# Block products from expert 2 of group 2 on: moving a stage border in an attention and mixture-of-experts kernel

## The chip, the cores and the metric

The kernel runs on one NeuronCore of a Trainium2 chip. Five engines work side by side, each through its own queue in order: TensorE (PE) multiplies matrices into PSUM, VectorE (DVE) and ScalarE (ACT) read PSUM and work element by element, GpSimd (POOL) works on SBUF alone, and SyncE (SP) issues DMAs. POOL issues DMAs too, on a queue of its own. The metric is device time in microseconds of one execution. The profile records one further execution of the program.

## What is computed

Attention through 32 memory slots for 8 batches, 8 heads, 576 rows and head size 64; its output, 4608 rows of 512, goes through four experts that are weighted by `domain_probs`:

```python
a = softmax(phi over s)                      # 8, 8, 576, 32
k_m, v_m = a^T k, a^T v                      # 32 x 64 for each head
attn = softmax(q k_m^T / 8 over the 32)      # 8, 8, 576, 32
x = attn v_m                                 # as 4608 x 512
for e in range(4):
    h = maximum(x @ w1[e], 0)                # 4608 x 1024
    out += p[:, e:e+1] * (h @ w2[e])         # 4608 x 512
```

Everything is float32. Each product is made of float32r parts: a number is split into a high part and the rest, and three matmuls (high by high, high by rest, rest by high) make one product.

## The kernel before

**Groups, experts, steps.** The rows are taken in 4 groups of 2 batches (9 tiles of 128 rows), each through 4 experts. The program numbers steps: an expert has `STEPS` = 32 of them, a group `PAIR` = 128. A step is one batch half of a group (256 or 320 rows) and one of the eight 128-wide parts `j` of the hidden size. Counting groups from 0 in the code, group 1 of the code is the second group, "group 2" of the title.

**A step.** `x @ w1` is never formed from x: v_m times w1 is made first (`vw`, 128 x 512 tiles of four heads), then `first` multiplies attention by `vw` (six matmuls, L641 to L643), applies the relu and splits h on ACT and DVE (L653, L655). `second` (L674 to L676) multiplies two row tiles, in every fourth half a third one (`hm`, the middle tile shared by two batches), by w2: three matmuls of 512 columns for each. `first` runs two steps ahead of `second`. `accumulate` adds to `acc` once in eight steps (L694, L696).

**A unit.** From step `BEGIN` on, `unit` takes the place of four steps. Four 128 x 256 blocks of the second product are made by 7 instead of 8 block products. That needs sums and differences of blocks of h (`x_out`, `y_diff`, `y_lo`, `y_last`, from the relu of `rows`, L916 to L918, on ACT, DVE and POOL) and of w2 (`sums`). Each of the 7 (`product`, L1002) is 2 x 3 matmuls of 256 columns; `add_in` (L1020) adds what stands in a product's bank to a quarter of `acc`, seven additions of 128 x 256 in a unit. Two banks (6 and 7) alternate for the products, banks 2 to 5 hold the rows, and two banks (0 and 1, "pm") are left for all else; the steps have four "pm" banks. `middle` (L1040 to L1042) does the shared middle tile as a step does.

**What feeds a unit.** The weights of four units (a block) are 8 tiles of 0.5 MB: four of w2 as split and kept in memory (`kw`), four of sums (`v`). SP loads them (`load_part`, L850) into a ring as the previous block frees its tiles, one in each of the first three units of a block and five in the last. `sums` makes the `v` tiles of one half of an expert: two loads of raw w2 on SP (L201), four operations on DVE a few steps later (L225 to L228), four casts on ACT (L213), four subtractions on POOL (L214) and four stores on POOL's queue (L219). Its raw tile is a buffer that the next job needs as well.

**The plan.** Everything else is hung on steps by `at(step, work)`, and `run_plan` emits it at the start of a step, ahead of that step's products; within an engine that is the order of execution. `ATT` gives each batch the step at which its phi is loaded, the step at which v is written, and the steps of its three score groups and three turns. From the first of these the phi softmax (+3 to +6), its transposes (+8 to +11) and kv products (+10 to +24) follow at fixed distances. A score group is L463 on PE, L473 and L476 on DVE, an exp on ACT and L490 to L493 on DVE; a turn transposes it on PE (L514) and splits it into `AT` (L525, L526). `JOBS` lists the sums: step, home of the raw tile, lag to the DVE part. Where the batches' v lies in memory order for four heads (`vs`), the `vw` of an expert is made for two groups at once (`four`, L579, through three `vst` buffers to `vwd` by POOL's queue, L567) and loaded back (`load_vw`, L618); for experts 1 and 2 of the first two groups it is made in place (`vw_mm`, `vw_out`, L554 and L556). PE, ACT and DVE wait for one another by semaphores; a buffer's next writer waits for its last reader.

The numbers that the change edits:

```python
SEVEN = 2
BEGIN = SEVEN * PAIR
UNITS = (NG - SEVEN) * E * 2 * 4
```

Of the kernel before, what the change touches and what calls it, by code (L numbers as in the profile page):

```python
# [19 lines left out]
P = 128  # L20
# [59 lines left out]
FIRST_LOADS = (PAIR + 112, PAIR + 121, PAIR + 122, PAIR + 123, PAIR + 124, PAIR + 125, PAIR + 126, PAIR + 127)  # L80
# [3 lines left out]
def body(ctx: ExitStack, tc: tile.TileContext, qm, qt, kv, kvt, phi, prob, w1, w1d, w2, out):  # L84
# [104 lines left out]
    def sums(s, home, lag, e, fh):  # L189
# [3 lines left out]
        sub, v = nc.vector.tensor_sub, nc.vector  # L193

# [8 lines left out]
        def high(i, j):  # L203
# [10 lines left out]
            nc.gpsimd.tensor_sub(kept[2][:, i, j], kept[i][:, j], kept[3 + i][:, j].bitcast(F32))  # L214
# [523 lines left out]
    def attention(b, s, written, scores, turns):  # L738
# [43 lines left out]
    for k in range(NG):  # L782
        for e in range(E):
# [38 lines left out]
    for n, job in enumerate(JOBS):  # L822
        sums(*job, n // 2, n % 2)
# [450 lines left out]
```

## Time and profile before

| | |
|---|---|
| time, median of 3 runs | 1392.94 us (1391.73 to 1395.49) |
| the profiled execution | 1392.14 us, of which its span 1390.3 us |
| granted TensorE clock over the span | 0.997 |
| moved by DMA | 301.37 MB, 217 GB/s on average |
| steps 128 to 255 | about 415.5 to 776.6 us of the span |
| first sixteen units | about 776.6 to 936.4 us |

A row of the groups view names line, engine, operation, output and input tiles and their shapes, then busy time and mean duration, then the idle time before and what ended it. A row of the timeline has start, duration, engine, line, operation, and in brackets the wait that went before. The waits view has who waited for what: total us, times, longest.

### The profile page before, as it was taken

To read this page: it belongs to the slowest core of one execution; us is meant where nothing else is said; L and a number is where in the kernel's file an instruction comes from. 1 tells how busy PE (TensorE), PEld (TensorE's weight loads), DVE (VectorE), ACT (ScalarE), POOL (GpSimd) and SP (SyncE) were. 2 spreads that over 40 slices of the span, in tenths; PEclk is the share of its full clock that TensorE was granted. 3 is DMA by queue.
4 is the path that set the end of the run, shared out by engine and by line. 5 is a ranking of instruction groups with operands and counts; after the bars stand their busy time and mean duration, and the time that the engine had idled before them with its cause. 6 is when DMAs were issued, how large, how long until landed. Compare 5 with 4: busy or idle time off the path is not lost.

```text
span 1390.3 us, 25223 instructions
## 1 busy us (share of the span) xinstructions
PE 1362.0 (98%) x8894; PEld 1248.4 (90%) x8894; DVE 841.3 (61%) x1894; ACT 625.4 (45%) x1536; POOL 617.4 (44%) x652
## 2 busy tenths in 40 slices
PE   7999999999999999999999999999999999999998
PEld 6788888788888888889888998999999999999998
DVE  7875535446755365454434467777767666666666
ACT  6765555443345465463344354555543333333332
POOL 4400354745353424433144375677753334443432
PEclk9999999999999999999999999999999999999999
DMA  6742354897675364354598898899984866666661
GB/s 255 240 165 76 117 182 173 311 322 240 210 281 212 107 229 146 125 203 143 178 290 296 277 321 292 286 344 311 326 298 131 259 186 177 180 173 175 175 181 75
DMA packets 102029, 301.37 MB, mean 217 GB/s; under 512 B 24976, under 2 KB 26128, under 8 KB 101904
## 3 DMA queue, kind: packets, MB, share of 16 engines
q1 hardware_dynamic: 81168, 224.26, 51.9%
q0 software_dynamic: 19584, 71.31, 13.0%
q10 hardware_dynamic: 1152, 4.19, 0.7%
q8 instruction: 71, 1.16, 0.3%
q14 instruction: 54, 0.44, 0.1%
HBM read 213.46 MB, written 84.93 MB: 215 GB/s over the span
## 4 chain that ended last, share of the span: by engine, by line
PE 89%; DVE 4%; DMA 2%; issue 2%; ACT 1%; SPq 0%; POOL 0%; DVEq 0%; ACTq 0%; POOLq 0%
PE banks L1002 22%; PE banks L676 9%; PE banks L674 9%; PE banks L675 9%; PE banks L916 5%; PE banks L917 5%; PE banks L918 5%; PE banks L641 5%; PE banks L642 4%; PE banks L643 4%; PE banks L579 3%; PE banks L463 2%; PE banks L357 2%; DMA stage<-in_w 1%; PE banks L1040 1%
## 5 line engine op out<-in xcount | busy, mean ns | idle before, releaser
L1020 DVE SCALAR_TENSOR_TENSOR acc<-banks,pt,acc 128x256 f32<-128x256 f32 x416 | 200.0, 481 | 107.7 <-PE banks L1002 104.2
L160 POOL TENSOR_TENSOR w<-stage,w 128x512 fp32r<-128x512 f32 x134 | 177.0, 1332 | 188.7 <-ACT w L159 179.4
L655 DVE SCALAR_TENSOR_TENSOR h<-banks,h 128x256 fp32r<-128x256 f32 x256 | 107.3, 420 | 168.6 <-ACT h L653 111.4
L676 PE MATMUL banks<-w,h 128*128 128x512 f32 x512 | 201.2, 393 | 3.4 <-DVE h L655 3.4
L674 PE MATMUL banks<-w,h 128*128 128x512 f32 x512 | 201.9, 394 | 0.1
L675 PE MATMUL banks<-w,h 128*128 128x512 f32 x512 | 201.4, 393 | 0.0
L653 ACT ACTIVATE h<-banks 128x256 fp32r<-128x256 f32 x256 | 98.0, 384 | 199.8 <-PE banks L643 169.9
L641 PE MATMUL banks<-AT,vw 128*128 128x256 f32 (+1 forms) x512 | 156.6, 306 | 3.7 <-DVE h L655 1.8
L1002 PE MATMUL banks<-w,a 128*128 128x256 f32 x1080 | 154.4, 282 | 0.3 <-DVE acc L1020 0.2
L643 PE MATMUL banks<-AT,vw 128*128 128x256 f32 (+1 forms) x512 | 150.9, 295 | 1.2 <-DVE vw L556 1.2
L916 PE MATMUL banks<-AT,vw 128*128 128x256 f32 (+1 forms) x512 | 151.6, 296 | 0.0
L642 PE MATMUL banks<-AT,vw 128*128 128x256 f32 (+1 forms) x512 | 151.3, 296 | 0.0
L917 PE MATMUL banks<-AT,vw 128*128 128x256 f32 (+1 forms) x512 | 151.1, 295 | 0.0
L918 PE MATMUL banks<-AT,vw 128*128 128x256 f32 (+1 forms) x512 | 150.9, 295 | 0.0
L1002 PEld LDWEIGHTS banks<-w,a 128*128 128x128 f32 x1080 | 143.6, 188 | 4.8 <-issue 0.9
L983 POOL TENSOR_TENSOR vt<-ph,vt 128x512 fp32r<-128x512 f32 x64 | 84.1, 1314 | 107.3 <-ACT vt L982 78.3
L676 PEld LDWEIGHTS banks<-w,h 128*128 128x128 f32 x512 | 96.3, 188 | 25.8 <-DVE h L655 4.3
L346 POOL TENSOR_TENSOR kvs<-stage,kvs 128x512 fp32r<-128x512 f32 x58 | 75.4, 1317 | 93.2 <-ACT kvs L345 87.3
L641 PEld LDWEIGHTS banks<-AT,vw 128*128 128x128 f32 x512 | 96.8, 189 | 13.8 <-DVE vw L556 3.8
L674 PEld LDWEIGHTS banks<-w,h 128*128 128x128 f32 x512 | 96.4, 188 | 12.0 <-ACT h L653 0.4
L675 PEld LDWEIGHTS banks<-w,h 128*128 128x128 f32 x512 | 96.4, 188 | 10.9
L159 ACT CAST w<-stage 128x512 fp32r<-128x512 f32 x168 | 102.7, 619 | 4.5 <-DMA stage<-in_w 2.1
(149 smaller groups left out, 2985.4 us busy)
## 6 DMA issues: line engine op xcount, KB each, us to landing
w<-kw SPq DMA_DIRECT2D x93, 512.0 KB, 5.5
vwd<-vst POOLq DMA_DIRECT2D x80, 512.0 KB, 6.4
vw<-vwd SPq DMA_DIRECT2D x320, 128.0 KB, 6.0
w<-v SPq DMA_DIRECT2D x55, 512.0 KB, 5.6
stage<-in_w SPq DMA_DIRECT2D x44, 512.0 KB, 4.5
stage<-in_w1d SPq DMA_DIRECT2D x40, 512.0 KB, 5.3
stage<-in_kv SPq DMA_DIRECT2D x32, 512.0 KB, 4.3
kw<-w POOLq DMA_DIRECT2D x24, 512.0 KB, 5.6
```

Of the source, the lines that this page charges most:

```text
L160: eng.tensor_sub(dst[:, 1, :], raw, dst[:, 0, :].bitcast(F32))
L641: nc.tensor.matmul(ps, w[:, 0, f], at_t[:, g, 0, c], start=g == 0, stop=False)
L642: nc.tensor.matmul(ps, w[:, 0, f], at_t[:, g, 1, c], start=False, stop=False)
L643: nc.tensor.matmul(ps, w[:, 1, f], at_t[:, g, 0, c], start=False, stop=g == 1)
L674: nc.tensor.matmul(po[t], x[:, 0, :], w[:, 0, :], start=j == 0, stop=False)
L675: nc.tensor.matmul(po[t], x[:, 0, :], w[:, 1, :], start=False, stop=False)
L676: nc.tensor.matmul(po[t], x[:, 1, :], w[:, 0, :], start=False, stop=j == NJ - 1)
L916: nc.tensor.matmul(ps, w[:, 0, f], at_t[:, g, 0, c], start=g == 0, stop=False)
L917: nc.tensor.matmul(ps, w[:, 0, f], at_t[:, g, 1, c], start=False, stop=False)
L918: nc.tensor.matmul(ps, w[:, 1, f], at_t[:, g, 0, c], start=False, stop=g == 1)
L1002: nc.tensor.matmul(ps, a[:, l, jj], w[:, r, c], start=start and jj + i == 0, stop=jj == 1 and i == 2, skip_group_check=True,)
L1020: VE.scalar_tensor_tensor(a, src, p, a, ALU.mult, ALU.add)
```

## The change

Units begin at step 192 (`PAIR + 2 * STEPS`, expert 2 of the second group) and not at 256: 80 units instead of 64. The attention of batches 4 to 7 has its phi and kv parts packed into steps 122 to 189; the scores of batches 4 and 5 come after it, among the units. The sums of experts 2 and 3 are made first; one job moves to step 74, where its subtractions are on DVE and not on POOL (`BUSY_POOL`), none is left at 119 or 154, and three stand at 190, 202 and 214, with the raw tile in an "AT" buffer. The last folds of batch 7 and the last `vw` tiles of the steps get tables of their own, and a tile that folds still need is taken for the units later (`open_last`).

```diff
 ATT = {
...
-    4: (PAIR + 2, PAIR + 37, (PAIR + 34, PAIR + 37, PAIR + 41), (PAIR + 38, PAIR + 42, PAIR + 45)),
+    4: (PAIR - 6, PAIR + 21, (PAIR + 69, PAIR + 81, PAIR + 85), (PAIR + 99, PAIR + 103, PAIR + 107)),
+    5: (PAIR + 8, PAIR + 35, (PAIR + 109, PAIR + 115, PAIR + 119), (PAIR + 117, PAIR + 123, PAIR + 127)),
...
-SEVEN = 2
-BEGIN = SEVEN * PAIR
-UNITS = (NG - SEVEN) * E * 2 * 4
+SEVEN = 1, 2
+BEGIN = SEVEN[0] * PAIR + SEVEN[1] * STEPS
+UNITS = (LAST - BEGIN) // 4
...
 JOBS = (
-    (62, "", 5), (86, "", 5), (97, "", 5), (108, "", 5), (119, "", 5),
-    (PAIR + 26, "AT", 4), (PAIR + 61, "a", 4), (PAIR + 87, "", 5),
+    (2, 0, 62, "", 5), (2, 1, 74, "", 5), (3, 0, 86, "", 5), (3, 1, 97, "", 5), (0, 0, 108, "", 5),
+    (0, 1, PAIR + 62, "AT", 4), (1, 0, PAIR + 74, "AT", 4), (1, 1, PAIR + 86, "AT", 4),
 )
+BUSY_POOL = (74,)
...
-FIRST_LOADS = (PAIR + 112, PAIR + 121, PAIR + 122, PAIR + 123, PAIR + 124, PAIR + 125, PAIR + 126, PAIR + 127)
+FIRST_LOADS = (-16, -7, -6, -5, -4, -3, -2, -1)
+LAST_PAIR_AT = (28, 29, 31, 32)
+LAST_FOLD = (PAIR + 56, PAIR + 61)
...
+        rest_on = nc.vector if s in BUSY_POOL else nc.gpsimd
...
-            nc.gpsimd.tensor_sub(kept[2][:, i, j], kept[i][:, j], kept[3 + i][:, j].bitcast(F32))
+            rest_on.tensor_sub(kept[2][:, i, j], kept[i][:, j], kept[3 + i][:, j].bitcast(F32))
...
-            for j in range(NJ if 0 < nk < SEVEN else 0):
+            for j in range(NJ if nk and s + STEPS < BEGIN else 0):
                 at(s + W2_AGAIN + j, lambda a=(nk, ne, j): load_w2(*a))
...
-                    when = VW_LOAD_AT if nk < SEVEN else VW_LOAD_7
+                    when = VW_LOAD_AT if s < BEGIN else VW_LOAD_7
...
+    def open_last():
         n = att.tile([P, 2 * P], F32, name="xs", tag="xs", bufs=2)
         ph2["n"] = n.rearrange("p (j c) -> p j c", j=2)
...
-        idle["pm"] = deque(range(2))
+        held_now = [n for tag, n, _ in lent.values() if tag == "pm"]
+        assert not set(held_now) & {2, 3}
+        idle["pm"] = deque(n for n in idle["pm"] if n < 2)
+        open_last()
```

Three places of the instruction queues show it. On PE, in expert 3 of the second group, before (a step; `w` is a tile of w2, `h` the relu's split):

```order
L643 MATMUL banks<-AT,vw 128x256
L674 MATMUL banks<-w_6901,h 128x512
L675 MATMUL banks<-w_6901,h 128x512
L676 MATMUL banks<-w_6901,h 128x512
L641 MATMUL banks<-AT,vw 128x256
```

and among the units of the same group now (`a` is the input of two of the seven products, L923 to L925 are the rows):

```order
L1009 MATMUL banks<-w_6200,a 128x256 x3
L1009 MATMUL banks<-w_6233,a 128x256 x3
L1009 MATMUL banks<-w_5732,a_6400 128x256 x3
L1009 MATMUL banks<-w_6026,a_6400 128x256 x3
L923 MATMUL banks<-AT,vw 128x256
L924 MATMUL banks<-AT,vw 128x256
```

Three matmuls of 512 columns for a row tile have given way to sixes of 256 columns.

On DVE, the first score group of batch 4, before, between steps (`mx` and `z` are its maximum and sum, `at` its softmax, `h` what the next `second` needs):

```order
L473 TENSOR_REDUCE mx<-banks 128x16
L476 TENSOR_TENSOR at<-banks,mx 128x512
L309 TENSOR_TENSOR a<-banks,a 128x2x4x64
L655 SCALAR_TENSOR_TENSOR h<-banks,h 128x256
L309 TENSOR_TENSOR a<-banks,a 128x2x4x64
```

and now the same group in a unit:

```order
L477 TENSOR_REDUCE mx<-banks 128x16
L480 TENSOR_TENSOR at<-banks,mx 128x512
L1027 SCALAR_TENSOR_TENSOR acc<-banks,pt,acc 128x256
L987 SCALAR_TENSOR_TENSOR a<-banks,a 128x512
L1027 SCALAR_TENSOR_TENSOR acc<-banks,pt,acc 128x256 x2
L997 SCALAR_TENSOR_TENSOR xs<-banks,ph 128x256
```

Behind the softmax there now stand the additions that empty the products' banks, and the splits for the next unit, where the split of `h` and of the phi transposes stood.

On POOL, around step 81, before (`vwd` stores a `vst` tile, `w` is a split of w1):

```order
L567 DMA vwd_2966<-vst 128x1024
L160 TENSOR_TENSOR w_2973<-stage,w_2973 128x512
L567 DMA vwd_2996<-vst 128x1024
L160 TENSOR_TENSOR w_3005<-stage,w_3005 128x512
L567 DMA vwd_3028<-vst 128x1024
L160 TENSOR_TENSOR w_3035<-stage,w_3035 128x512
```

and now:

```order
L571 DMA vwd_3008<-vst 128x1024
L163 TENSOR_TENSOR w_3017<-stage,w_3017 128x512
L223 DMA v_3020<-sv 256x1x512
L223 DMA v_3020<-raw 256x1x512
L571 DMA vwd_3046<-vst 128x1024
L163 TENSOR_TENSOR w_3053<-stage,w_3053 128x512
L571 DMA vwd_3088<-vst 128x1024
L163 TENSOR_TENSOR w_3097<-stage,w_3097 128x512
L223 DMA v_3100<-sv 256x1x512
L223 DMA v_3100<-raw 256x1x512
```

Two pairs of stores of the sums (`sv` and `raw` hold the parts) stand between the stores of the four-head products.

More of the change, by code (lines that the diff above doesn't have):

```diff
@@ L187, in load_w2, with sums @@
         w2t[k, e, j] = t
-    def sums(s, home, lag, e, fh):
+    def sums(e, fh, s, home, lag):
         kept = []
@@ L760, in attention @@
             at(s + 13 + 3 * hp, lambda hp=hp: kv_out(b, hp))
-        for g in range(2):
-            at(s + 18 + 6 * g, lambda g=g: [kv_fold(b, 2 * g + i) for i in range(2)])
-            at(s + 19 + 6 * g, lambda g=g: kv_pick(b, g))
+        for g, n in enumerate(LAST_FOLD if b == B - 1 else (s + 18, s + 24)):
+            at(n, lambda g=g: [kv_fold(b, 2 * g + i) for i in range(2)])
+            at(n + 1, lambda g=g: kv_pick(b, g))
         at(written, lambda: v_split(b))
@@ L810, in body @@
                 for odd in range(2 if by_four else 0):
-                    when = VW_LOAD_AT if nk < SEVEN else VW_LOAD_7
+                    when = VW_LOAD_AT if s < BEGIN else VW_LOAD_7
                     at(s + when[odd][fh], lambda a=(nk, ne, odd, fh): load_vw(*a))
                 for g in range(0 if by_four else 2):
+                    when = LAST_PAIR_AT if fh and s + STEPS == BEGIN else PAIR_AT[fh]
                     for i, u in enumerate(units_w1(ne, fh, g)):
                         at(s + PAIR_W1[fh][2 * g + i], u)
-                        vw_steps(s + PAIR_AT[fh][2 * g + i], nk, ne, fh, 2 * g + i, (0, 1))
+                        vw_steps(s + when[2 * g + i], nk, ne, fh, 2 * g + i, (0, 1))
     for b in range(2, B):
@@ L821, in body @@
             at(e * STEPS + KEEP_AT[e] + j, lambda a=(e, j): keep_w2(*a))
-    for n, job in enumerate(JOBS):
-        sums(*job, n // 2, n % 2)
+    for job in JOBS:
+        sums(*job)
     for s in FIRST_LOADS:
-        at(s, lambda: load_part(wp.tile([P, 2, DM], F32R, name="w2", tag="w2", bufs=NJ + 1)))
+        at(BEGIN + s, lambda: load_part(wp.tile([P, 2, DM], F32R, name="w2", tag="w2", bufs=NJ + 1)))
     early = [("kv", 0, 0), ("kvt", 0)] + [("kv", 0, hp) for hp in range(1, NP)]
@@ L842, in parts, with place_of @@
             yield ("v", e, fh, i), (2 + i // 2, i % 2)
+    def place_of(u):
+        k, r = divmod(u + BEGIN // 4, 2 * E * 4)
+        e, r = divmod(r, 8)
+        fh, pair = divmod(r, 4)
+        return k, e, fh, pair // 2, pair % 2
     for block in range(UNITS // 4):
-        e, fh = divmod(block % (2 * E), 2)
+        _, e, fh, _, _ = place_of(4 * block)
         waiting += [(block, *x) for x in parts(e, fh)]
@@ L861, in free @@
                 ring.extend(W[u // 4][i, jj] for jj in range(2))
-    def place_of(u):
-        k, r = divmod(u, 2 * E * 4)
-        e, r = divmod(r, 8)
-        fh, pair = divmod(r, 4)
-        return SEVEN + k, e, fh, pair // 2, pair % 2
     ph2 = {}
```

5 lines of the change are left out of this document (2 added, 3 removed).

## The prediction

> **What bounds the kernel now.** I read the page first: busy time by engine, then the shares of the chain that ended last.
>
> ```profile
> PE 1362.0 (98%) x8894; PEld 1248.4 (90%) x8894; DVE 841.3 (61%) x1894; ACT 625.4 (45%) x1536; POOL 617.4 (44%) x652
> PE 89%; DVE 4%; DMA 2%; issue 2%; ACT 1%; SPq 0%; POOL 0%; DVEq 0%; ACTq 0%; POOLq 0%
> ```
>
> TensorE (PE) is busy 98% of the span of 1390.3 us and carries 89% of the chain. Its busy time isn't yet its peak, so the second view is the windows of the stages that the change touches. The rows are steps 128 to 191 and 192 to 255 of the plan, the first sixteen of the block-product units, and four units without attention.
>
> ```profile
> core 0: us, PE busy (x) PEld busy (x) DVE busy (x) ACT busy (x) POOL busy (x), PEclk, DMA share, GB/s
> 415.50:605.60 190.10, 186.56 (x1074) 163.60 (x1073) 93.79 (x227) 98.97 (x258) 75.09 (x64) 1.00 0.49 171
> 605.60:776.60 171.00, 171.00 (x960) 149.99 (x959) 80.12 (x188) 66.76 (x186) 58.19 (x60) 1.00 0.72 226
> 776.60:936.40 159.80, 158.00 (x1165) 151.01 (x1164) 112.30 (x250) 79.87 (x176) 106.51 (x120) 1.00 0.90 306
> 1102.20:1137.70 35.50, 35.50 (x279) 34.99 (x278) 23.11 (x53) 11.95 (x29) 14.06 (x16) 1.00 0.68 202
> ```
>
> In steps 192 to 255 PE never rests: 171.00 of 171.00 us. This is the stage that is rewritten. It can get shorter only by fewer or narrower matmuls. VectorE (DVE) has room there (80 of 171 us); a quiet unit uses 23.11 of 35.50 us, 65%. So the price of a matmul is the first term, and DVE the first suspect for what comes back.
>
> **What a matmul costs.** The timeline of PE gives starts; neighbouring starts give the price, since a matmul's own length overlaps the next.
>
> ```profile
> 705.85 0.40 PE L674 MATMUL banks<-w,h 128*128 128x512 f32 x1
> ...
> 707.22 0.28 PE L641 MATMUL banks<-AT,vw 128*128 128x256 f32 x1
> 1130.56 0.88 PE L1002 MATMUL banks<-w,t 128*128 128x256 f32 x6
> 1131.27 0.88 PE L1002 MATMUL banks<-w,tl 128*128 128x256 f32 x6
> ...
> 1132.69 1.60 PE L1002 MATMUL banks<-w,a 128*128 128x256 f32 x12
> 1134.13 0.28 PE L916 MATMUL banks<-AT,vw 128*128 128x256 f32 x1
> ```
>
> Six matmuls of 512 columns stand between 705.85 and 707.22 (L674 to L676, twice): 1.37 / 6 = 0.228 us. Six of 256 columns take 0.71 us, 0.118; twelve take 1.44 us, 0.120. I use 0.119. A narrow one costs 52% of a wide one, not 50%.
>
> **Part 1: the products.** Sixteen groups of four steps become sixteen units. Four steps hold 4 x 2 x 3 = 24 wide matmuls; a unit holds 7 x 6 = 42 narrow ones. The first product and the shared middle tile keep their matmuls. So 16 x 24 = 384 wide ones go (384 x 0.228 = 87.6 us) and 16 x 42 = 672 narrow ones come (672 x 0.119 = 80.0 us): **-7.6 us**. With 0.118 and 0.120 at the ends: -8.3 to -7.0. All of it lies on the path, as PE has no rest there.
>
> The TensorE page of the Trainium skill (TensorE: Matmul & The Clock Gate, section "Wait — 56ns, not 53.3ns?") makes a warm matmul N / 2.4 GHz plus 2.5 ns; by that estimate 384 x 215.8 ns go and 672 x 109.2 ns come, -9.5 us. The rows here are 6 to 9% dearer than that at both widths, and the sum goes by the rows.
>
> **Part 2: a wait that goes.** Of the idle 3.5 us in steps 128 to 191, the waits and the timeline name this:
>
> ```profile
> PE banks L641 <- DVE h L655: 1.8, 1, 1.8
> PE banks L641 <- DVE vw L556: 1.7, 3, 0.9
> 516.45 0.39 PE L641 MATMUL banks<-AT,vw 128*128 128x256 f32 x1 [1.83 <-DVE h L655]
> ```
>
> At 516 us, step 162, batch 4's first scores, batch 5's exp and normalisation, the w2 sums loaded at step 154 and the vw tiles of the next expert all stand on DVE and ScalarE within three steps. Afterwards the scores stand at 197 and later, and these sums at 190 or later. The stretch from 121 to 189 has the same phi and kv work per step as before, no scores and no sums. I take **-1.8 us**; ends 0 (something else is late there) and -3.5 (the three vw waits go too, which I don't expect: vw tiles are written at the same steps but two).
>
> **Part 3: scores inside units.** Batches 4 and 5 now do their six score groups and six turns among units 1 to 15. What a group costs there is shown by batches 6 and 7, whose scores already stand in units (840 to 1070 us). First PE's waits, then those of its weight loads:
>
> ```profile
> PE banks L1002 <- DVE acc L1020: 1.9, 4, 1.2
> PE banks L463 <- DVE AT L526: 0.3, 1, 0.3
> PEld banks L1002 <- DVE acc L1020: 2.6, 3, 1.5
> PEld banks L1002 <- issue: 0.7, 2, 0.4
> PEld banks L463 <- DVE AT L526: 0.5, 1, 0.5
> PEld banks L463 <- DVE accm L1052: 0.3, 1, 0.3
> PEld banks L1040 <- DVE at L476: 0.2, 1, 0.2
> ```
>
> Behind a waiting matmul stands the whole PE queue: a product's bank must be emptied by an accumulation on DVE, and that stands behind softmax. Two batches cost 2.2 us of PE idle, or 4.3 us counted at the weight loads. The new two get the same six groups: **+3.0 us**, ends 2.2 and 4.3. Their turns stand 4 or more steps after the softmax (group 3 of batch 6 has one step), which speaks for the middle and not the upper end.
>
> **Part 4: sums inside units.** Three of the eight jobs now run in units 0 to 7, none before. Durations, of DVE, by line:
>
> ```profile
> L493 DVE TENSOR_TENSOR at<-at,z 128x512 f32<-128x512 f32 x16 | 14.8, 922 | 0.4
> L476 DVE TENSOR_TENSOR at<-banks,mx 128x512 f32<-128x512 f32 x16 | 11.0, 690 | 0.5
> L473 DVE TENSOR_REDUCE mx<-banks 128x16 f32<-128x512 f32 x16 | 10.9, 682 | 1.4 <-PE banks L463 1.4
> L490 DVE TENSOR_REDUCE z<-at 128x16 f32<-128x512 f32 x16 | 10.8, 676 | 0.5 <-ACT at L483 0.5
> L226 DVE TENSOR_TENSOR raw<-raw 128x512 f32<-128x512 f32 x8 | 7.5, 936 | 0.3
> ```
>
> A score group is about 0.68 + 0.69 + 0.68 + 0.92 = 3.0 us of DVE and costs 3.0 / 6 = 0.5 us of PE; a job is four operations of 0.7 to 0.9 us, about 3.2 us, in two pairs. So 0.35 to 0.5 each: **+1.0 us** for three, ends 0 and 1.6. DVE itself isn't full: in 16 units 16 x 23.11 / 4 = 92 us, plus 6 x 3.0, plus 3 x 3.2, plus six AT subtractions of about 0.7 (as L476) and the 16 vst subtractions that move along, also 0.7: some 135 us in about 160. That is more than the 112 us of 159.8 in the windows row above, and the rival below.
>
> **Part 5: the job at step 74.** It is new in the stretch in which the four-head products go to memory (steps 72 to 87). It adds four casts on ScalarE, eight operations on DVE (its four low parts are on VectorE there) and four stores on POOL's queue, each ahead of a vwd store. That queue once cost PE this, shown by the waits of ScalarE and by windows:
>
> ```profile
> ACT vst L584 <- DMA vwd<-vst: 15.4, 5, 7.5
> 268.70:271.60 2.90, 0.42 (x2) 0.00 (x1) 0.69 (x1) 1.41 (x5) 0.21 (x1) 1.00 0.93 380
> 271.60:275.80 4.20, 3.55 (x11) 2.98 (x12) 2.54 (x7) 3.09 (x9) 4.16 (x5) 0.59 0.56 113
> 297.70 1.29 POOL L160 TENSOR_TENSOR w<-stage,w 128x512 fp32r<-128x512 f32 x1 [1.60 <-ACT w L159]
> ```
>
> A vst buffer (there are three) was free only after 7.5 us; PE idled about 2.5 of 2.9 us, then ran at a granted clock of 0.59 for 4.2 us (4.2 x 0.41 = 1.7). So 4.2 us is the upper end. At steps 80 to 84 POOL rests 1.60 us of each 3.4 us step, and two more issues fit in that; a 7.5 us wait gave 2.5 us of idle, so 5 us are absorbed. I take **0**, ends 0 and 4.2. The new raw load on SP stands among w1d loads which wait for POOL longer than it does; it hides there.
>
> The SBUF page of the Trainium skill (SBUF — State Buffer, section "Who interferes with whom") says that a VectorE operation with two SBUF inputs blocks against a GpSimd operation reading SBUF, for the whole instruction. L493 and L226, which have such inputs, average 922 and 936 ns against 690 ns of L476, whose input is PSUM, so the trace agrees; by it the four subtractions moved to VectorE at step 80 would take up to 4 x 1.3 us (one POOL operation each) longer, which the 5 us still cover.
>
> Other edits (the second kv fold of batch 7 one step earlier, the last two vw tiles one step later, the "n" tile opened later, first loads by offset, 32 more weight loads of 0.5 MB on SP against 16 w2 reloads gone): 0, hidden as long as PE has rows and products queued; the DMA share of 0.90 in 776 to 936 us, with PE busy 158.00 of 159.80, is the row for that load.
>
> **Sum**, against the profiled execution's own 1392.14 us (span 1390.3, 1.84 around it; the median of the runs, 1392.94, is 0.06% off): -7.6 - 1.8 + 3.0 + 1.0 + 0 = -5.4, so **1386.7 us**.
>
> **Rivals.**
>
> *The step-74 job repeats the vst stall* (Part 5's upper end): -5.4 + 4.2 gives 1391. For: three buffers, and two stores ahead of a vwd store. Against: the rest on POOL.
>
> *DVE fills in units 0 to 15*: 135 us in 160 leaves 15%, and where softmax, sums and a vst subtraction meet, the accumulation is late at each. If each of six groups and three jobs costs 1 us, Parts 3 and 4 are +9 instead of +4: 1391.7.
>
> *SP stands still behind a sums load; slower.* A raw tile can be loaded only when the previous job's stores have landed:
>
> ```profile
> SPq L201 <- DMA v<-raw: 39.5, 4, 17.8
> ```
>
> Four times SP waited, 9.9 us on average and 17.8 at most. In units the same SP queue loads the product weights behind that, at the end of every fourth unit, about one unit (9 us) ahead of use. The loads at steps 202 and 214 come three steps (7 us) after the previous store is issued. Should SP wait more than 9 us there, PE idles for the rest: two waits of 17.8 give 2 x 8.8 = 17.6, so -5.4 + 17.6 = 1404. Here the gap is three steps and not one, so I hold it unlikely.
>
> *Weight loads set the spacing; slower.* If a narrow matmul cost over 87.6 / 672 = 0.130 us, Part 1 would turn sign; at the 0.188 us that a weight load lasts (L1002 PEld below) it is +39, so 1429.
>
> ```profile
> L1002 PEld LDWEIGHTS banks<-w,a 128*128 128x128 f32 x1080 | 143.6, 188 | 4.8 <-issue 0.9
> ```
>
> The starts above exclude it: 0.118 to 0.120. The same TensorE page, section "Back-to-back issue gap", gives 81 ns at 128 and 131 ns at 512 columns for load and matmul pairs; on a line between these 256 columns are an estimated 98 ns, and the change would add 15 us. The trace disagrees with both figures.
>
> *More waits go*: the vw waits too (-1.7) and Parts 3 and 4 at their lower ends (+2.2): 1383.
>
> **Chances.** Forecast 0.55, step-74 stall 0.14, full DVE 0.15, SP 0.07, weight loads 0.01, more waits go 0.08. Within 0.3% of 1392.9 means 1388.8 to 1397.1, about what a measurement of this kernel can tell from no change. Faster: 0.55 and 0.08, less a little at the forecast's edge, 0.61. Same: 0.14 + 0.15 and that edge, 0.31. Slower: 0.08. The range takes in the unknown costs' ends and the two rivals near 1391, and leaves out the SP case: 1381 to 1393.
>
> **What would show it.** Part 1: units 0 to 15 at 42 products each, the quiet ones in about 8.9 us; part 2: no wait of L641 on h near step 162; parts 3 and 4: L1002's successor waiting for the accumulation, 3 to 5 us in the first sixteen units; part 5: no wait of PE in steps 80 to 88. A slow clock, a product waiting for a weight DMA, or PE idle over 5 us in units 0 to 15 would make the prediction wrong.

## The result: slower by 21.5 us, and the profile after

| | before | after |
|---|---|---|
| median (4 runs each, side by side) | 1392.69 us (1391.73 to 1395.49) | 1414.22 us (1413.12 to 1415.76) |
| ratio, with its 95% interval | 1 | 1.0152 (1.0134 to 1.017) |
| profiled execution | 1392.14 us | 1414.01 us |
| granted TensorE clock over the span | 0.997 | 0.992 |

The forecast was 1386.7 us, with a range up to 1393. The busy times and the chain of the changed kernel come first, as they did before:

```profile
PE 1366.3 (97%) x9182; PEld 1260.9 (89%) x9182; DVE 894.7 (63%) x1996; ACT 647.2 (46%) x1552; POOL 669.9 (47%) x712
PE 82%; DVE 7%; DMA 5%; ACT 2%; issue 2%; POOL 1%; SPq 1%; DVEq 0%; ACTq 0%; POOLq 0%
```

PE carries 82% of the chain and no longer 89%; DVE, DMA and ACT took the rest. The windows of the same stages (steps 128 to 191, units 0 to 15, the next sixteen units; columns as before: start and end, length, then PE, its loads, DVE, ACT, POOL, granted clock, DMA share, GB/s) tell where:

```profile
422.00:616.00 194.00, 188.61 (x1079) 164.23 (x1078) 87.12 (x219) 102.92 (x273) 72.66 (x59) 1.00 0.43 144
616.00:790.90 174.90, 162.23 (x1183) 153.82 (x1182) 126.27 (x275) 77.21 (x171) 101.87 (x113) 0.98 0.74 249
790.90:951.00 160.10, 157.73 (x1180) 151.25 (x1180) 116.68 (x260) 79.27 (x178) 109.03 (x123) 1.00 0.95 322
```

Steps 192 to 255 took 171.00 us without a rest. The sixteen units in their place take 174.90 us, of which PE rests 12.7, at a mean clock of 0.98. The units after them are as long as they were (160.10 for 159.80 us).

To split this further, the start of each matmul is set against the next one's, and the median of its line and width is taken off: what is left is lost to waits and to a slow clock. The sums in us, each stage counted from the product that `first` makes for its first step, which runs two steps ahead (so that 128 to 135 in the table is done while the plan is at steps 126 to 133), or from the first rows of its first unit (192 to 203 in the table are units 0 to 2, and so on; below, stretches of steps and units are counted in this way):

| steps | before | after |
|---|---|---|
| start, 0 to 3 | 2.0 | 4.2 |
| 76 to 91 | 5.1 | 7.9 |
| 92 to 107 | 2.3 | 3.8 |
| 128 to 135 | 0.7 | 4.0 |
| 136 to 191 | 3.6 | 3.9 |
| 192 to 203 | 0 | 8.3 |
| 204 to 267 | 0.3 | 13.2 |
| all others | 12.6 | 12.9 |
| **sum** | **26.6** | **58.2** |

So 31.6 us more are lost. PE's own work fell: by the medians 384 wide matmuls of 0.231 went and 672 narrow ones of 0.118 came, -9.4 us. Together that makes 22.2 us, where the two profiled executions are 21.9 us apart. Two rows are taken as chance: in the other kernels that were run the start lost 2.0 to 2.7, and steps 92 to 107 lost about 2.3 or about 3.8, with or without the change.

PE's waits between 600 and 800 us (who waited for whom: us, times, longest; before there was none from 605.6 to 776.6 us):

```profile
PE banks L923 <- DVE v L400: 3.7, 1, 3.7
PE banks L1009 <- DVE acc L1027: 3.6, 7, 1.4
PE banks L583 <- POOL w L163: 2.1, 1, 2.1
PE banks L467 <- DVE AT L530: 1.8, 1, 1.8
PE banks L1009 <- issue: 1.4, 2, 1.2
```

Rows of the first unit wait for batch 7's fold, products for the accumulation, a four-head product for GpSimd, scores for a turn. The experiments take them one by one.

### The profile page after: what moved, and what is told of

Same layout as the page of the kernel before. It is cut to its first block, busy times and chain, and to the rows that moved or that the text cites. A ratio compares the mean times of both kernels' runs of the same rounds, so it can differ in the third digit from the quotient of the medians.

```text
span 1412.2 us, 26074 instructions
## 1 busy us (share of the span) xinstructions
PE 1366.3 (97%) x9182; PEld 1260.9 (89%) x9182; DVE 894.7 (63%) x1996; ACT 647.2 (46%) x1552; POOL 669.9 (47%) x712
## 4 chain that ended last, share of the span: by engine, by line
PE 82%; DVE 7%; DMA 5%; ACT 2%; issue 2%; POOL 1%; SPq 1%; DVEq 0%; ACTq 0%; POOLq 0%
PE banks L1009 26%; PE banks L680 6%; PE banks L678 6%; PE banks L679 6%; PE banks L923 6%; PE banks L924 5%; PE banks L925 5%; PE banks L645 3%; PE banks L646 3%; PE banks L647 3%; PE banks L467 2%; PE banks L583 2%; PE banks L361 2%; PE banks L1047 1%; PE banks L1048 1%
## 5 line engine op out<-in xcount | busy, mean ns | idle before, releaser
L1027 DVE SCALAR_TENSOR_TENSOR acc<-banks,pt,acc 128x256 f32<-128x256 f32 x528 | 253.5, 481 | 131.9 <-PE banks L1009 127.1
L163 POOL TENSOR_TENSOR w<-stage,w 128x512 fp32r<-128x512 f32 x134 | 177.8, 1338 | 154.3 <-ACT w L162 142.0
L1009 PE MATMUL banks<-w,a 128*128 128x256 f32 x1344 | 193.3, 282 | 1.0 <-DVE acc L1027 0.7
L923 PE MATMUL banks<-AT,vw 128*128 128x256 f32 (+1 forms) x640 | 190.2, 297 | 3.7 <-DVE v L400 3.7
L924 PE MATMUL banks<-AT,vw 128*128 128x256 f32 (+1 forms) x640 | 189.6, 296 | 0.0
L925 PE MATMUL banks<-AT,vw 128*128 128x256 f32 (+1 forms) x640 | 189.4, 296 | 0.0
L1009 PEld LDWEIGHTS banks<-w,a 128*128 128x128 f32 x1344 | 179.2, 189 | 6.8 <-issue 1.8
L680 PE MATMUL banks<-w,h 128*128 128x512 f32 x384 | 151.8, 395 | 4.0 <-DVE h L659 4.0
L678 PE MATMUL banks<-w,h 128*128 128x512 f32 x384 | 152.3, 397 | 1.2 <-ACT h L657 0.7
L679 PE MATMUL banks<-w,h 128*128 128x512 f32 x384 | 151.4, 394 | 0.0
L975 ACT ACTIVATE a<-banks 128x512 fp32r<-128x512 f32 x80 | 47.9, 599 | 174.1 <-DVE ph L981 131.3
L923 PEld LDWEIGHTS banks<-AT,vw 128*128 128x128 f32 x640 | 121.1, 189 | 4.6 <-issue 4.1
L1000 POOL TENSOR_TENSOR tl<-xs,tl 128x256 fp32r<-128x256 f32 x80 | 59.7, 747 | 131.8 <-ACT tl L999 66.6
L924 PEld LDWEIGHTS banks<-AT,vw 128*128 128x128 f32 x640 | 121.3, 190 | 0.1
L925 PEld LDWEIGHTS banks<-AT,vw 128*128 128x128 f32 x640 | 121.0, 189 | 0.0
L645 PE MATMUL banks<-AT,vw 128*128 128x320 f32 (+1 forms) x384 | 117.9, 308 | 2.0 <-DVE vw L560 1.9
L1009 PE MATMUL banks<-w,vt 128*128 128x256 f32 x768 | 113.8, 280 | 4.2 <-DVE acc L1027 2.9
L647 PE MATMUL banks<-AT,vw 128*128 128x320 f32 (+1 forms) x384 | 113.2, 296 | 1.3 <-DVE vw L560 1.3
```

Of the source, the lines that this page charges most:

```text
L163: eng.tensor_sub(dst[:, 1, :], raw, dst[:, 0, :].bitcast(F32))
L645: nc.tensor.matmul(ps, w[:, 0, f], at_t[:, g, 0, c], start=g == 0, stop=False)
L647: nc.tensor.matmul(ps, w[:, 1, f], at_t[:, g, 0, c], start=False, stop=g == 1)
L678: nc.tensor.matmul(po[t], x[:, 0, :], w[:, 0, :], start=j == 0, stop=False)
L679: nc.tensor.matmul(po[t], x[:, 0, :], w[:, 1, :], start=False, stop=False)
L680: nc.tensor.matmul(po[t], x[:, 1, :], w[:, 0, :], start=False, stop=j == NJ - 1)
```

## The experiments

Each kernel ran beside the kernel before; compared are the ratios to it (its own median lay between 1392.7 and 1394.3 us from one set of runs to the next) and the lost time by the table's rows. The changed kernel's ratio is 1.0152.

### The packing alone

```diff
-SEVEN = 1, 2
+SEVEN = 2, 0
```

> The changed kernel's attention and sums places, but units only from step 256, as before: the packing alone. Theory A (the packing costs in the steps, at 74 to 104 and 121 to 160): lost time up to step 192 stays as in the changed kernel, about 8 us over before without the start, so 1399 to 1402 us. Rival (the steps swallow it, and the whole loss is made by units from 192 on): 1392 to 1395 us.

Measured: 1401.13 us, ratio 1.0041 (1.0026 to 1.0057). Steps 76 to 91 lost 7.0 and 128 to 135 lost 3.7 us, and from 192 to 267 only 0.2. So the packing costs 0.4%, in two places ahead of 192, and the rest of the loss, 1.1%, is made by the units from 192 on, where the same work stands among units.

### Batch 4's phi

On SP's queue the changed kernel loads phi among the reloads of w2, and DVE stands for it (start, length, engine, line, and in brackets the wait ahead):

```profile
408.81 3.84 SPq L189 DMA_DIRECT2D w<-kw  x3
412.83 1.79 SPq L264 DMA_DIRECT2D ph<-in_phi  x2
...
422.75 0.75 DVE L269 TENSOR_REDUCE nm<-ph 128x1 f32<-128x576 f32 x1 [2.49 <-DMA ph<-in_phi]
...
424.60 0.75 DVE L269 TENSOR_REDUCE nm<-ph 128x1 f32<-128x576 f32 x1 [0.91 <-DMA ph<-in_phi]
...
426.05 0.50 PE L539 MATMUL banks<-w,vt 128*128 128x512 f32 x1 [1.81 <-DVE h L659]
```

The load was issued at 412.83, and its first half was there at 422.75, ten microseconds later, behind three reloads of 0.5 MB. The relu's split stands behind that maximum on DVE, a vw matmul waits for the bank.

```diff
-        at(s, lambda: load_phi(b))
+        at(s - 3 if b == 4 else s, lambda: load_phi(b))
```

> The changed kernel with batch 4's phi loaded at step 119 and not at 122, ahead of the eight w2 reloads on SP's queue instead of among them; nothing else moves. Theory A (the 1.8 us wait at 424 us, and those behind it, come from phi landing 10 us after its issue, so that DVE stands at the maximum ahead of the relu's split): lost time of steps 126 to 133 falls from 4.0 to about 1 us, the median by 3 to 1411 us. Rival (the vw tiles and phi need DVE at once, whenever phi lands): lost time stays above 3 us, 1414 us.

Measured: 1409.6 us, ratio 1.0113 (1.0094 to 1.0132). The same DVE row, now without a wait:

```profile
404.26 1.26 SPq L264 DMA_DIRECT2D ph<-in_phi  x1
...
417.53 0.75 DVE L269 TENSOR_REDUCE nm<-ph 128x1 f32<-128x576 f32 x1
```

Steps 128 to 135 lost 0.8 us for 4.0: the late load was the cause, worth 3.2 us by lost time.

### The job at step 74

```diff
     for job in JOBS:
-        sums(*job)
+        if job[:2] != (2, 1):
+            sums(*job)
```

> The changed kernel without the sums job at step 74: the sums of the second half of expert 2 are not made, and the units load the first half's in their place. Theory A (the job's stores and casts repeat the vst stall): the 5.2 us that PE loses in steps 80 to 83 go, the 5.3 us of before come back in steps 76 to 79 instead of 1.9, so about 2 to 3 us less, 1411.5 us. Rival (the stall belongs to the four-head products alone and moves by itself): 1414, within 1 us of the changed kernel.

Measured: 1408.57 us, ratio 1.011 (1.008 to 1.014). Steps 76 to 91 lost 2.7 us for 7.9. One profile says little here, since this stall varies: in the twelve profiles of kernels with the job these steps lost 6.9 to 8.9 us, 7.8 on average, and in the eight without it 2.6 to 6.9, 4.8 on average. The job costs 3.0 us on average. The ratio fell by more, 0.42% or 5.9 us, but its interval for the kernel without the job, four runs from 1405.9 to 1413.0 us, is wide.

### The border: four orders

The first theory was that batch 7's fold, whose bank the rows of the first unit need, comes too late. First the fold and all of batches 6 and 7 were put two steps earlier:

```diff
-    6: (PAIR + 24, PAIR + 51, ...
+    6: (PAIR + 22, PAIR + 49, ...
-    7: (PAIR + 38, PAIR + 64, ...
+    7: (PAIR + 36, PAIR + 62, ...
-LAST_FOLD = (PAIR + 56, PAIR + 61)
+LAST_FOLD = (PAIR + 54, PAIR + 59)
```

> The changed kernel with the phi and kv parts of batches 6 and 7 two steps earlier, so that batch 7's last fold stands at step 187 and its pick at 188, not 189 and 190. Theory A (the 3.7 us wait of the rows at the border, and the slow clock behind it, come from that pick being late): 3.7 + 1.6 to 3.2 us go, 1408 to 1409 us, and no wait of the rows on v in the trace. Rival (the queues of DVE and ACT are full there whatever stands in them, and the vw tile or the first unit's splits are late next): at least 1412 us.

Measured: 1415.53 us, ratio 1.0148 (1.0124 to 1.0172). The theory fell. The rows wait as before, for the next in line:

```profile
PE banks L923 <- DVE vw L560: 2.8, 1, 2.8
```

Of 8.3 us lost in units 0 to 2, 5.9 stayed, and 3.4 more were lost in steps 136 to 191, into which batches 6 and 7 are now packed more closely. Then the vw tiles were moved as well, in two ways:

```diff
-LAST_PAIR_AT = (28, 29, 31, 32)
+LAST_PAIR_AT = (26, 27, 29, 30)
...
```

> The kernel with batches 6 and 7 two steps earlier, and in addition the last four vw tiles at steps 186, 187, 189 and 190 (not 188, 189, 191 and 192), the last two in banks 0 or 1, which the units keep: neither a fold nor a vw tile then holds a bank that the first unit's rows need. Theory A (the border costs what meets at it): the 3.0 us wait of the rows and most of the 1.5 us one behind goes, with the slow clock, 4 to 6 us less than 1415.5: about 1410.5 us. Rival (ScalarE's first casts for the units, behind which the rest stands, set the border): 1414 us or more.

Measured: 1424.18 us, ratio 1.0215 (1.0189 to 1.0242), with 12.9 us lost in steps 136 to 191 and 10.2 in units 0 to 2. Part of it was a flaw of the edit: at 186 and 187 the previous pair's tiles stand already, so two shared a step.

```diff
-LAST_PAIR_AT = (28, 29, 31, 32)
+LAST_PAIR_AT = ((18, 19, 25, 26), (27, 28, 29, 30))
...
```

> Batches 6 and 7 two steps earlier, and the last six vw tiles one a step: 185, 186, then 187 to 190 (not 186, 187, then 188, 189, 191, 192), the one at 190 in bank 0 or 1. No two tiles share a step, no fold or vw tile holds a bank of the first unit's rows, and only one vw tile is written after the first unit's casts. Theory A: the 3.0 us wait of the rows, the 1.5 us in unit 0 and the slow clock go, 4 to 6 us less than 1415.5: about 1410.5 us. Rival (any vw tile beside the first unit's casts on ACT and DVE costs its 3 us): 1414 us or more.

Measured: 1419.19 us, ratio 1.0186 (1.0168 to 1.0204): without the flaw still worse than with the tiles where they were (1415.53), with 12.9 us lost in units 0 to 2. In both, the last vw matmul waits for the bank that the tile before it holds (4.2 us in the first of the two):

```profile
PE banks L539 <- DVE vw L560: 4.2, 1, 4.2
```

So neither the fold nor a tile was the cause by itself; each is only what stands last. What stands ahead of them shows in the timeline of ScalarE at the border of the changed kernel, and of those who wait for it:

```profile
617.59 0.60 ACT L957 ACTIVATE ph<-banks 128x512 f32<-128x512 f32 x1 [2.37 <-PE banks L925]
618.22 0.41 ACT L966 CAST a<-ph 128x256 fp32r<-128x256 f32 x1
618.68 0.41 ACT L969 CAST t<-ph 128x256 fp32r<-128x256 f32 x1
619.11 1.17 ACT L558 CAST vw<-banks 64x512 fp32r<-64x512 f32 x2
620.18 0.42 ACT L398 COPY kT<-banks 64x64 f32<-64x64 f32 x2
620.62 0.42 ACT L398 COPY v<-banks 64x64 f32<-64x64 f32 x2
...
618.22 0.42 DVE L965 SCALAR_TENSOR_TENSOR ph<-banks,ph 128x256 f32<-128x256 f32 x1 [2.54 <-ACT ph L957]
620.31 1.39 DVE L560 TENSOR_TENSOR vw<-banks,vw 64x512 fp32r<-64x512 f32 x2 [1.67 <-ACT vw L558]
...
622.08 0.45 DVE L400 TENSOR_TENSOR v<-v,banks 64x64 f32<-64x64 f32 x2
...
622.68 0.36 PE L923 MATMUL banks<-AT,vw 128*128 128x256 f32 x1 [3.73 <-DVE v L400]
```

ScalarE stands 2.37 us for the first unit's first rows, since the relu of these rows (L957) was emitted ahead of the work of step 190. The vw casts and the fold's copies stand behind it, though PE had done the matmuls that they read by 614.1 us. VectorE stands as well, 2.54 us for that relu (L965, also emitted ahead of step 190's work) and then 1.67 for the vw cast, and PE waits for banks until 622.68. Its clock pays once more:

```profile
624.00:626.50 2.50, 2.50 (x11) 2.21 (x10) 0.52 (x2) 0.60 (x1) 0.00 (x0) 0.52 0.00 0
```

After 3.73 us of rest the granted clock was 0.52 in this stretch, and its matmuls take the longer for it. The last edit changes only where the first unit's X is made: the relu and two casts on ScalarE, and with them the operation L965 on VectorE and two subtractions on GpSimd:

```diff
-        x_relu(0)
-        x_out(0)
         steps(BEGIN - 2, BEGIN - 1)
+        x_relu(0)
+        x_out(0)
```

> The changed kernel with one thing in another order: the first unit's relu and casts of X (L957 to L970) are emitted behind step 190's work and not ahead of it, so that ScalarE does that step's vw casts and the fold's copies while it would wait for the first rows. Theory C (the rows' 3.7 us wait at 618.6 us comes from ScalarE standing 2.4 us for the first rows with those casts queued behind; border and border2 put more casts into that queue and got worse): the wait falls under 1 us and the slow clock behind it goes, 4 to 5.5 us less, 1409 to 1410 us. Rival (the chain of casts for the first unit is the length that counts, one step later it keeps the first product waiting instead): 1413 us or more.

Measured: 1407.97 us, ratio 1.0113 (1.0091 to 1.0135). The waits of PE from 605 to 660 us and the clock of the first units are now:

```profile
PE banks L1009 <- DVE acc L1027: 2.0, 4, 1.4
...
612.80:628.00 15.20, 13.81 (x92) 12.59 (x91) 10.75 (x24) 8.50 (x21) 5.42 (x7) 1.00 0.43 151
```

No wait of the rows is left, and the clock stays at 1.00. Units 0 to 2 lost 3.0 us for 8.3. This order at the border was worth 5.3 us; ScalarE's and VectorE's share of it are not separated, as both stood for the same rows. Of the 3.0 left, 1.4 are one wait behind a vw tile, and about 1 is the first sums job, as the next kernel suggests, in which the border keeps the order of the changed kernel.

### Sums and scores among units

```diff
     for job in JOBS:
-        sums(*job)
+        if job[2] < PAIR:
+            sums(*job)
```

> The changed kernel without the three sums jobs at 190, 202 and 214: the sums of the second half of expert 0 and of expert 1 are not made, and those of expert 0's first half are loaded in their place. As the prediction had it (0.35 to 0.5 us each): about 1 us less, 1413. Theory A (the third job holds POOL when the four-head products begin at 224, 2.2 us, and DVE's share comes on top): 3 to 4 us less, 1410.5, and no wait of the four-head product on POOL. Rival (the scores fill DVE, the jobs are nothing): 1414.

Measured: 1408.4 us, ratio 1.0101 (1.0074 to 1.0128). The wait for POOL is gone, 1.0 us less is lost in units 0 to 2 and 3.8 less in units 3 to 18: 4.8 us for three jobs, where the prediction had 1.0.

```diff
+        if b in (4, 5):
+            at(scores[0], lambda: st.update({("AT", b): st["AT", b - 2]}))
+            return
         for t0, n in zip((0, 2, 4), scores):
```

> The changed kernel without scores and turns of batches 4 and 5: the units of the third group take the attention of batches 2 and 3. PE's own work falls by 2 x (20 x 0.111 + 10 x 0.11) = 6.6 us. As the prediction had it (3.0 us of waits): 1414.2 - 9.6 = 1404.5 us. Theory A (9.4 us lost in units 3 to 18 beside the jobs' share, nearly all by these scores beside the four-head products): 13 to 15 us less, 1400 us. Rival (the units lose this time by themselves): 1407.

Measured: 1394.51 us, ratio 1.0012 (0.9997 to 1.0027). Units 3 to 18 lost 4.7 us for 13.2. The expectation counted PE's own work too low: a score matmul shows twice, so a batch has 40 of 0.111 and 10 transposes of 0.11 us, 11.1 for two. The rest, 8.5 us, is time lost to waits and to the slow clock behind them (units 12 to 15 lost 0.1 us for 6.6), which the six groups and turns make and for which the prediction had 3.0.

Part of this comes from GpSimd; how much is not separated. Rows of DVE and GpSimd in unit 13 of the changed kernel:

```profile
756.44 2.21 DVE L495 TENSOR_SCALAR z<-z 128x16 f32<-128x16 f32 x1
...
756.62 1.31 POOL L163 TENSOR_TENSOR w<-stage,w 128x512 fp32r<-128x512 f32 x1
757.87 0.74 POOL L967 TENSOR_TENSOR a<-ph,a 128x256 fp32r<-128x256 f32 x1
...
777.80 1.66 DVE L497 TENSOR_TENSOR at<-at,z 128x512 f32<-128x512 f32 x1
```

The addition to z has 16 columns, and its median is 0.175 us; here it ends with the second GpSimd operation (758.61). The plainest case was in the kernel before all along:

```profile
334.44 5.19 DVE L491 TENSOR_SCALAR z<-z 128x16 f32<-128x16 f32 x1
...
334.10 5.49 POOL L160 TENSOR_TENSOR w<-stage,w 128x512 fp32r<-128x512 f32 x4
```

It ends at 339.63, with the last of four GpSimd operations (339.59). In the changed kernel's units it is the four-head splits on GpSimd (L163) that meet batch 5's softmax, which stood in steps before.

```diff
-        nc.vector.tensor_scalar_add(zv[:, :, 0], zv[:, :, 0], 1e-9)
```

> The changed kernel without the addition of 1e-9 to the softmax sums z of the scores (L495; each z is at least 1, since the maximum is subtracted, so that the float32 sum doesn't change). Theory B (this 128x16 addition, 0.17 us by itself, stands on VectorE until GpSimd's running operations end: 2.21 us at 756.4 us, up to 5.2 us near step 100; the four-head splits on GpSimd now meet batch 5's softmax): the stalls at step 102 and units 13 to 15 shrink, 3 to 5 us less, 1409 to 1411 us. Rival (the multiplication L497 behind it, with two inputs in SBUF, takes the same wait: it took 1.66 for 0.69 us at 777.8): 1 us less or nothing, 1413 to 1414.

Measured: 1406.95 us, ratio 1.0099 (1.0083 to 1.0114). The median favours theory B, the rows favour the rival. Of the 7.3 us between the two profiled executions, 3.0 stand in the two rows taken as chance above (2.7 for 4.2 and 2.3 for 3.8). The multiplication takes the wait; these are rows of the kernel before without the addition (in the changed kernel without it, the same operation took 2.44 us at 751.68):

```profile
331.18 5.90 DVE L492 TENSOR_TENSOR at<-at,z 128x512 f32<-128x512 f32 x1
...
331.03 5.49 POOL L160 TENSOR_TENSOR w<-stage,w 128x512 fp32r<-128x512 f32 x4
```

Units 12 to 15 lost 3.2 us less, but 3.2 came back at 799 us, where weights landed late, and 2.7 less were lost behind unit 18. Of this gain one part is the same in all profiles: in steps 288 to 299, among the last scores and turns of batch 6, the sixteen kernels with the addition lost 2.4 to 2.8 us, and the four without it 1.2. So leaving it out takes 1.2 to 1.6 us away there, while the meeting with GpSimd stays.

### Three edits at once

The edits of phi and of the border together, and with them other places of the jobs:

```diff
-    (0, 1, PAIR + 62, "AT", 4), (1, 0, PAIR + 74, "AT", 4), (1, 1, PAIR + 86, "AT", 4),
+    (0, 1, PAIR + 60, "AT", 4), (1, 0, PAIR + 70, "AT", 4), (1, 1, PAIR + 80, "AT", 4),
...
+        at(s - 3 if b == 4 else s, lambda: load_phi(b))
...
         steps(BEGIN - 2, BEGIN - 1)
+        x_relu(0)
+        x_out(0)
```

> Three edits of the changed kernel at once: batch 4's phi at step 119 (measured -4.6), the first unit's X behind step 190's work (theory C: -4 to -5.5), and the sums jobs of the units at 188, 198 and 208 instead of 190, 202 and 214, so that the third is off GpSimd when the four-head products begin at 224 (2.2 us). Theory A and C (the causes stand at separate places and add up): 1401 to 1404 us. Rival (what is saved at one place is lost at the next): 1407 us or more.

Measured: 1406.52 us, ratio 1.0101 (1.0082 to 1.0119), between the theory and the rival. Against the kernel with the border's edit alone, phi gave 2.9 us and the third job 3.2, as expected. But the other two jobs, two and four steps earlier, met a vw tile near the border and a softmax in unit 6; units 1, 6 and 7 lost 8.3 us more. A job has a price where it stands.

Then the jobs where they were, and the addition left out:

```diff
-        nc.vector.tensor_scalar_add(zv[:, :, 0], zv[:, :, 0], 1e-9)
...
+        at(s - 3 if b == 4 else s, lambda: load_phi(b))
...
         steps(BEGIN - 2, BEGIN - 1)
+        x_relu(0)
+        x_out(0)
```

> The changed kernel with the three edits that took a measured loss away, each alone: the first unit's X behind step 190's work (-6.2), batch 4's phi at step 119 (-4.6 by the medians, 3.0 by lost time), no addition of 1e-9 (-7.3 by the medians, 2.5 to 4 by lost time beyond the start). Theory (separate places, so they add up; jobs and scores among units stay): 1400 to 1403 us, still 7 to 10 over before. Rival (they share what they save): 1405 us or more.

Measured: 1401.71 us, ratio 1.0057 (1.0039 to 1.0074). That is 0.95% under the changed kernel; the three alone gave 0.39, 0.39 and 0.53%, together 1.31%. They add up for the larger part, and the kernel stays 0.6% over before.

### A later border

With units only from expert 3, attention can stand where it stood before, and nothing but rows meets at the border. Five versions differ in the places of the sums jobs; the last job can't stand at 215 any more, since the units take its buffers. The first diff below shows the lines that count, the others show what differs from the first version:

```diff
-SEVEN = 1, 2
+SEVEN = 1, 3
...
+    (1, 1, PAIR + 10, "AT", 4), (2, 0, PAIR + 26, "AT", 4), (2, 1, PAIR + 61, "a", 4),
```

> Units from step 224 (expert 3 of the second group) with the attention of batches 4 to 7 at the places of before (batch 5's three turns among units 5 to 7), the sums of expert 3 first and no job at 74. Theory A (a border costs only what meets there; products gain half as much, 8 x (24 x 0.228 - 42 x 0.119) = 3.8 us): 1388 to 1391 us. Rival (a border away from the group's end costs 5 us or more by itself, or DVE fills in units): 1395 us or more.

Measured: 1395.87 us, ratio 1.0014 (1.0001 to 1.0028). The first three units lost 0.3 us: here a border cost nothing by itself. The eight units saved 3.5 us by the difference of the two profiles, and the steps gave 4.0 back. Of these, 2.4 stand at 148: the job at 138 holds the kvs buffers, ScalarE waits for its stores, and PE behind it. The other 1.6 are a slow clock behind the wait at 162: the granted clock was 0.50 from 523 to 525 us. The profile of the kernel before has the same wait and a clock of 1.00 behind it; that of the kernel before without the addition to z has the slow clock (0.50 from 516 to 518 us, and 1.6 us lost). The row of ScalarE's waits:

```profile
ACT kvs L349 <- DMA v<-sv: 6.9, 1, 6.9
```

```diff
-    (1, 1, PAIR + 10, "AT", 4), (2, 0, PAIR + 26, "AT", 4), ...
+    (1, 1, PAIR + 0, "AT", 4), (2, 0, PAIR + 14, "AT", 4), ...
```

> Units from step 224 with the attention of before, and the two sums jobs in AT buffers at steps 128 and 142, not 138 and 154. Theory A (the stalls at steps 148 to 151 and 162 are made by the sums' work on DVE beside kv, scores and vw): 2.4 us and 1.6 to 3.6 us less than the 1395.9 of the kernel with 138 and 154: 1390 to 1392, just faster than before. Rival (the wait at step 162 belongs to the scores and vw tiles alone, the jobs cost wherever they are): 1394 to 1396.

Measured: 1396.75 us, ratio 1.0026 (1.001 to 1.0042). The 1.9 us wait at step 162, which the prediction had put down to the sums, is gone with the job that stood at 154, and so is the one at 148. But the job at 128 waits 6.2 us for its raw tile, which lands behind the w2 reloads, and costs 5.9. Products also waited for weights at the border, and 6.1 us were lost in units 0 to 2. This profile is of the longest of ten executions (1404.0 us; the others took 1395.1 to 1398.8), so most executions can't have had all of that. The rows of VectorE's and PE's waits:

```profile
DVE raw L229 <- DMA raw<-in_w: 6.2, 1, 6.2
...
PE banks L1009 <- DMA w<-v: 3.5, 3, 1.8
```

```diff
+    (1, 1, PAIR + 26, "AT", 4), (2, 0, PAIR + 61, "a", 4), (2, 1, PAIR + 85, "a", 3),
```

> Units from step 224 with attention and sums of before; only the last job stands at 213 instead of 215, with its raw tile in the a buffer and three steps to its DVE part. Theory A (steps as before, a border where neither folds nor vw tiles stand costs nothing, eight units save 3.5 us): 1389 to 1391 us. Rival (the last job's stores hold the a tile, which the first unit's Y needs, and PE waits): 1393 us or more.

Measured: 1396.94 us, ratio 1.002 (1.0005 to 1.0035). The rival's mechanism: the a buffer is still being stored when the first unit writes its Y there, and unit 1 lost 4.7 us. The row of ScalarE:

```profile
705.72 0.60 ACT L975 ACTIVATE a<-banks 128x512 fp32r<-128x512 f32 x1 [4.21 <-DMA v<-raw]
```

```diff
+    7: (PAIR + 62, PAIR + 88, ...
...
+    (1, 1, PAIR + 14, "AT", 4), (2, 0, PAIR + 61, "a", 3), (2, 1, PAIR + 83, "a", 3),
```

> Units from step 224 as in the version with the last job at 213, but that job at 211 and batch 7 two steps earlier, so that its stores are done before the first unit's Y; and the AT job at step 142, where the scores of batch 4 aren't near. Theory A (the 3.1 us wait of the first unit's product and the stall at step 162 go): 1390 to 1392 us, 0.1 to 0.3% under before. Rival (the jobs cost wherever they stand in these steps): 1394 us or more.

Measured: 1401.31 us, ratio 1.0063 (1.0047 to 1.0079). The wait at 162 went, and units 0 to 2 lost 2.9 us for 4.7 (3.2 less in unit 1, 1.4 more in unit 2). But the job at 142 cost 1.9 at step 152, and batch 7's phi now waits 6.8 us for the stores from the same buffer near step 200, where 9.2 us were lost. The row of ScalarE's waits:

```profile
ACT a L312 <- DMA v<-raw: 6.8, 1, 6.8
```

```diff
+    (1, 1, PAIR + 2, "AT", 7), (2, 0, PAIR + 26, "AT", 4), (2, 1, PAIR + 61, "a", 4),
...
-        nc.vector.tensor_scalar_add(zv[:, :, 0], zv[:, :, 0], 1e-9)
```

> Units from step 224, attention of before, no addition of 1e-9; the AT jobs at steps 130 (with seven steps to its DVE part, since its raw tile landed late with four) and 154, the last job at 189. Theory (eight units save 3.5 us, the addition 2.5, the job at 130 costs 1 or less with its data there): 1388 to 1391 us, faster than before and than before without the addition. Rival (a job beside phi and kv costs its 2 to 6 us wherever it stands): 1393 us or more.

Measured: 1400.78 us, ratio 1.0051 (1.003 to 1.0071). The job at 130 finds its data there but no buffer: kv work has taken the three kvs buffers, and 11 us were lost at steps 140 to 147. The row of ScalarE:

```profile
462.06 0.62 ACT L217 CAST sv<-raw 128x512 fp32r<-128x512 f32 x1 [9.63 <-DMA v<-sv]
```

So no version with more units beat the kernel before. The one small gain needs no additional units:

> The kernel before, only without the addition of 1e-9 to z. Theory B (lost time behind unit 18 fell from 8.1 to 9 us in all other kernels to 5.9 without it): 2 to 3 us less than before, 1390 to 1391.5 us. Rival (the multiplication takes the wait, what fell was chance): within 1 us of before.

Measured: 1390.84 us, ratio 0.998 (0.9967 to 0.9993), about 2 us under before, the only kernel here whose interval lies below 1. In its profile steps 288 to 299 lost 1.2 us for 2.7, the gain that came with every kernel without the addition.

## Why the prediction was wrong, by its steps

**Part 1 was right.** The products came out at -9.4 us by the medians, for -7.6, since the median wide matmul takes 0.231 us and not the 0.228 of the six that were read; a unit with 256 rows and nothing beside it took 7.83 us, four such steps took 8.35.

**"Other edits ... 0, hidden as long as PE has rows and products queued" is the step that failed.** It priced the last fold and the last vw tiles by themselves, one step here or there, and took PE's queue for cover. At the border PE has nothing queued but rows that need those banks, and ScalarE and VectorE have the work that frees them queued behind a relu that waits for PE. This cost 7.3 us in units 0 to 2 (8.3 with the first sums job), of which the place of the first unit's X was 5.3. PE rested 12.7 us in the sixteen units and its clock fell to 0.52, two of the signs by which the prediction said that it would be wrong. No rival spoke of it; "slower" was given 0.08 for other mechanisms: SP behind a sums load, and dearer narrow matmuls, of which neither came: products of the changed kernel waited 0.5 us for weights, and a narrow matmul took 0.118 us.

**Part 2 was half right.** The wait at step 162 belonged to the sums job and went: in the versions with the later border it is there with a job at 154 and gone without one. But steps 136 to 191 lost 3.9 us for 3.6, so the 1.8 us were not gained: PE now waited 1.0 us with phi's transposes (L304) for a vw tile, and 0.7 with L678 for ScalarE's h. And "the same phi and kv work per step as before" left out the load: batch 4's phi was moved in among eight reloads, 3.2 us.

**Part 3 had the right mechanism at the wrong size:** 8.5 us for 3.0. The price came from batches 6 and 7, averaged over all their groups. Among the new ones, the 1.66 us multiplication at 777.8 and the 2.21 us addition at 756.4 stood beside four-head splits.

The Trainium skill (SBUF — State Buffer, section "Who interferes with whom") says that a VectorE instruction contends with GpSimd when it has two inputs in SBUF or runs in a two-port mode, which plain tensor_scalar can enter, and that the later of the two blocks fully. The prediction applied that to step 80 alone. The addition at 334.44 and, without it, the multiplication at 331.18 agree: each began just behind the first of four GpSimd operations, and they took 5.19 us for 0.175 and 5.90 for 0.69. DVE did not come in between any two of the four operations either. The row at 756.44 is listed 0.18 us ahead of GpSimd's, so it doesn't show who was the later.

**Part 4 too:** 4.8 us for 1.0. It counted DVE's operations, and not the GpSimd subtractions and stores ahead of a four-head split (2.1 us of PE at once), nor the place of a DVE operation ahead of an accumulation.

**Part 5** was 3.0 us on average, inside its bounds of 0 and 4.2, for the 0 that was taken; the rival of the vst stall was nearer. Two sums of the prediction are off without bearing on the forecast: 4 x 1.3 us is 5.2, which 5 us don't quite cover, and the rival with dear weight loads comes to 1433 us with the other terms, not 1429.

The sum by the measured sizes: products -9.4, border 7.3, scores 8.5, jobs 4.8, phi 3.3, steps 76 to 91 2.8 in these two profiles, the rest of the rows 1.2, and chance 3.7, which makes 22.2. The rival at 1391.7, DVE full in these units, pointed at the stage in which scores and jobs lost 13 us. But DVE was busy for 72% of it (126.27 of 174.90) and not full; what part of the 13 us is the order of work on DVE and what part is GpSimd's is not separated.

Left open: why steps 76 to 91 lose 2.6 to 6.9 us in the profiles of kernels without the job at 74, and what part of the 8.5 us the turns have. A version of the changed kernel with the scores away from the four-head splits wasn't tried, nor one that moves the first unit's X on ScalarE or VectorE alone.

## What to carry to other kernels

Price a moved border by what each in-order engine has queued there: an operation that waits for the other side, emitted early, holds up work whose inputs are long there. A resource that looks free on average (a queue, three buffers, VectorE at 72%) has to be checked at the very step to which work is moved, with the loads that the step issues. When taking the named wait away only changes its name, look at what stands ahead of both.

## What the runs showed of the hardware

A DVE operation of 16 columns took 5.19 us beside four GpSimd operations in a row, 30 times its median, and when it was left out the multiplication behind it took 5.90. The clock of TensorE was granted at 0.52 for 2.5 us behind 3.73 us of rest; behind 1.8 us of rest at step 162 it was granted at 0.50 in two profiles, and at 1.00 in that of the kernel before. A load of 288 KB took ten microseconds to land behind 1.5 MB of reloads on the same queue, where the median of such loads in that profile was 5.3.
